# Two kept heads per task: K tiles that hold half of each head, V in 8 KB rows, V 22 positions behind

## The chip, the cores and the metric

The kernel runs on one core of a Trainium2 chip. The metric is device time in microseconds of one execution, taken as the median over several runs. Before the change it is 1160.93 us (three runs, 1159.95 to 1161.16). One execution was also recorded by the hardware profiler; that execution took 1159.96 us, and its trace spans 1157.8 us from the first to the last instruction.

A core has five engines that work side by side, each through its own instructions in order: TensorE (PE, whose weight loads are listed apart as PEld), VectorE (DVE), ScalarE (ACT), GpSimd (POOL) and SyncE (SP). SP issues every DMA of this kernel. Sixteen DMA engines carry each transfer: a tile of 128 partitions is 128 rows, eight rows to an engine, and one row that is contiguous in DRAM shows as one packet of that size.

## The reference

The reference is two layers of a decoder for one new token of each of 8 sequences. The same caches and weights serve both layers:

```python
def _A_ref(x, k_cache, v_cache, wq, wo):        # x [8,1,512], caches [8,8,8192,128] bf16
    q = (x @ wq) ...                             # 32 query heads of 128; 4 of them share a KV head
    scores = einsum("bhqd,bhkd->bhqk", q, k) * (Dh ** -0.5)
    p = softmax(scores, axis=-1)
    o = einsum("bhqk,bhkd->bhqd", p, v)
    return o.reshape(B, Sq, Hq * Dh) @ wo
def _B_ref(x, w1, w2):
    return silu(x @ w1) @ w2                     # 512 -> 1792 -> 512

x = x + _A_ref(layernorm(x), k, v, wq, wo)
x = x + _B_ref(layernorm(x), w1, w2)
x = x + _A_ref(layernorm(x), k, v, wq, wo)
x = x + _B_ref(layernorm(x), w1, w2)
```

The K cache and the V cache hold 134 MB each. Every KV head of every sequence is 2 MB of K and 2 MB of V, for 8192 keys.

## The kernel before

**Tasks and positions.** The work is cut into 128 tasks, one for each layer, sequence b and KV head g. A task has four granules k of 2048 keys; a granule of K or of V is 512 KB, that is 4 KB on each partition. The program is written out by one loop over positions `p`, eight to a task, so a granule is two positions. In each position the loop emits, in a fixed order, what is due there for several tasks at once: query preparation (`emit_q`), transposes of K (`emit_t_until`, one ahead), scores (`emit_s`), the product of probabilities and V (`emit_pv`, `LP` = 14 positions behind the scores), the steps that fold the result (`emit_own`, `emit_join`, `emit_fold`, `emit_norm`), the softmax of an earlier task in phases of its eight positions, one step of the chain that leads from one layer to the next (output projection, MLP, query projection), and at last the DMA issues that may go out (`issue_until`).

**The arena.** K and V go to an arena of `NSLOT` = 28 slots of 512 KB. `plan_loads` sorts all loads by the position that needs them and gives each a slot; `after` is the position at which the slot's old content has been used. SP issues in that order and waits before each issue until the engines have in fact let go of the slot.

**Kept heads.** `KEEP` = 20 granules, K of heads 3 to 7, are loaded once for a sequence and stay in the arena from layer 0 to layer 1. They arrive as 2 MB transfers (`READ` = 4) with 16 KB on each partition. Heads 0 to 2 are not kept: their K is loaded in both layers in 512 KB transfers. V is never kept: all of it is loaded in both layers, as 512 transfers of 512 KB with rows of 4 KB. `make_tasks` puts some five or six tasks of heads 0 to 2 (of the next sequence's layer 0, of the last sequence's layer 1) between a sequence's kept tasks of layer 0 and those of layer 1, so that the chain from layer to layer has time. While these stream, 20 of the 28 slots hold kept K.

**Scores and softmax.** After 32x32 transposes on DVE the 128 partitions are four quarters that hold different keys. The query block `QB` has 16 columns, four for each quarter, so that one pass over K gives the scores of four query heads for all quarters. The scores of a task fill one PSUM bank (`SCp`, 128 x 512). The softmax takes the row maximum (`softmax_max`), joins it over the partitions on POOL, shifts and exponentiates on ACT into `P` (`softmax_exp`), sums (`softmax_sum`), transposes `P` on PE and copies it out (`emit_pt`), each in its phase of the task that follows. `P` shares its memory, `E`, with the fold of the output (`joint`).

The lines of the profile that the text uses: L105 a wait of SP for an engine, L379 the issue of a DMA, L497 transposes of K, L563 scores, L574 row maximum, L579 join of the maximum, L586 shift, L590 exponential, L597 and L599 the sum, L608 transposes of `P`, L612 the copy out, L628 product with V, L651 and L665 the fold.

Of the kernel before, what the change touches and what calls it, by code (L numbers as in the profile page):

```python
# [19 lines left out]
READ = (1, 1, 1, 4, 4, 4, 4, 4)  # L20
KEEP = 20
LT = 1
PRE = 10
LP = 14
EARLY = 4
DEAL_AT = 30
WO_FROM = 36
NTP = 2
NSCP = 2
NPT = 1  # L30
# [12 lines left out]
NAT = 2  # L43
CW = 32
# [108 lines left out]

def make_tasks(nb, nkv, keep_from):


    first = int(keep_from)
    a = [[(0, b, g) for g in range(first)] for b in range(nb)]
    kept = [[(0, b, g) for g in range(first, nkv)] for b in range(nb)]
    c = [[(1, b, g) for g in range(first, nkv)] for b in range(nb)]  # L160
    d = [[(1, b, g) for g in range(first)] for b in range(nb)]
    ahead = [t for b in range(1, nb) for t in a[b]]
    behind = []
    tasks = a[0] + kept[0]
    na = 0
    for b in range(nb):
        if b:
            tasks += kept[b]
        size = -(-(2 * first * (nb - 1)) // nb) if b in (0, nb - 1) else 2 * first * (nb - 1) // nb
        must = max(0, first * min(b + 1, nb - 1) - na)  # L170
        nd = size if b == nb - 1 else min(len(behind), first, size - must)
        tasks += behind[:nd]
        del behind[:nd]
        take = ahead[na:na + size - nd]
        na += len(take)
        tasks += take
        if b + 1 == nb:
            tasks += behind
        tasks += c[b]
        behind += d[b]  # L180
    assert na == len(ahead)
    return tasks + d[nb - 1]


def plan_loads(tasks, kept, nslot, ngran):
# [3 lines left out]
    for i, (layer, b, g) in enumerate(tasks):  # L189
        for k in range(ngran):  # L190
# [8 lines left out]
            loads.append(Load("V", b, g, k, i0 + GPG - 1 + LP, i0 + GPG - 1 + LP))  # L199
    loads.sort(key=lambda d: (d.need, d.kind))  # L200
# [8 lines left out]
    for d in loads:  # L209
        w = ngran if d.kind == "K" and (d.g, d.k) in kept else 1  # L210
        if w > 1 and d.k:
# [9 lines left out]
        for m in range(w):  # L221
            free[d.slot + m] = d.free
        if w > 1:
            whole[d.g] = d.slot
# [19 lines left out]
def _build(ctx, nc, A_x, A_k_cache, A_v_cache, A_wq, A_wo, B_w1, B_w2, out):  # L244
# [43 lines left out]
    def half(slot, h):  # L288
# [8 lines left out]
    XT = [sb([128, KT, B], BF16, f"XT{n}") for n in range(3)]  # L297
# [5 lines left out]
    QT2 = [sb([128, HQ], BF16, "QT2") for _ in range(2)]  # L303
# [12 lines left out]
    hsT = sb([128, FT * B], BF16, "hsT")  # L316
    xnT = sb([128, KT, B], BF16, "xnT")
    s1 = sb([128, B], FP32, "s1")
    s1a = sb([128, B], FP32, "s1a")
    s2 = sb([128, 1], FP32, "s2")  # L320
    s2a = sb([128, 1], FP32, "s2a")
    top = sb([128, REP], FP32, "top")
    tops = sb([128, REP], FP32, "tops")
    ssm = [sb([128, REP], FP32, "ssm") for _ in range(NST)]
    ssa = [sb([128, REP], FP32, "ssa") for _ in range(NST)]
    widths = {"own_q": NQ, "hm": REP, "far": REP, "mine": REP, "own_x": XW, "real": 1, "rowmax": 1,
              "eps": 1, "shift": 1, "eh": FT, "vr": B, "yr": B, "tr": B}
    widths.update({f"rcp{n}": REP for n in range(NST)})
    widths.update({f"rs{n}": 1 for n in range(NST)})
    row = sb([128, sum(widths.values())], FP32, "row")  # L330
    tiny, at_col = {}, 0
    for name, w in widths.items():
        tiny[name] = row[:, at_col:at_col + w]
        at_col += w
    own_q, hm, far, mine, own_x, real, rowmax, eps, shift, vr, yr, tr = (
        tiny[n] for n in ("own_q", "hm", "far", "mine", "own_x", "real", "rowmax", "eps", "shift", "vr", "yr", "tr"))
    rcp = [tiny[f"rcp{n}"] for n in range(NST)]
    rs = [tiny[f"rs{n}"] for n in range(NST)]

# [58 lines left out]
    def issue(d):  # L398
        cache = A_k_cache if d.kind == "K" else A_v_cache
        if d.kind == "K":  # L400
            src = cache[d.b, d.g].rearrange("(p k c) d -> k p (c d)", k=NGRAN // d.wide, p=128)[d.k // d.wide]
        else:
            src = cache[d.b, d.g].rearrange("(k p c) d -> k p (c d)", k=NGRAN, p=128)[d.k]
# [7 lines left out]
    with nc.Block() as block:  # L411

        @block.sync
        def _(sync_eng):
# [13 lines left out]
                    hm[:, :], lanes.rearrange("p c (k r) -> p r c k", k=NGRAN), AX.XY, ALU.add),  # L428
                reads=["ident"], writes=["hm"],
            )  # L430
            op(
# [7 lines left out]
            for n in range(NSCP):  # L439
                op(dve, lambda n=n: dve.memset(SCp[n][:, :], 0.0), writes=[f"SC{n}"])  # L440
            op(dve, lambda: dve.tensor_reduce(real[:, :], hm[:, :], AX.X, ALU.add), reads=["hm"], writes=["real"])
# [3 lines left out]
            op(dve, lambda: dve.tensor_scalar(  # L445
                far[:, :], hm[:, :], real[:, 0:1], FAR, op0=ALU.subtract, op1=ALU.mult),
               reads=["hm", "real"], writes=["far"])
# [57 lines left out]

            span_of = {}
# [10 lines left out]
            def emit_queries(layer, b):  # L517
                if layer == 0:
                    q, rq = QT1[:, b * HQ:(b + 1) * HQ], f"QT1_{b}"
                else:  # L520
                    q, rq = QT2[b % 2][:, :], f"QT2_{b % 2}"
# [9 lines left out]
            def emit_q(ti):  # L531
                layer, b, g = tasks[ti]
                if ti == span_of[(layer, b)][0]:
                    emit_queries(layer, b)
                n = ti % NQB
                at = qset[(layer, b)] * NPART * HQ
                op(dve, lambda: dve.tensor_tensor(  # L537
                    QB[n][:, :, :].rearrange("p i (a r) -> p i a r", a=NQ),
                    QSp[:, at:at + NPART * HQ].rearrange("p (i h) -> p i h", h=HQ)[:, :, g * REP:(g + 1) * REP].unsqueeze(2)
                    .to_broadcast([128, NPART, NQ, REP]),  # L540
                    own_q[:, :].unsqueeze(1).unsqueeze(3).to_broadcast([128, NPART, NQ, REP]), ALU.mult),
                   reads=["QS", "own_q"], writes=[f"QB{n}"])

            def emit_s(i):
# [9 lines left out]
                bank, qn = ti % NSCP, ti % NQB  # L554
# [17 lines left out]
            def softmax_max(ti):  # L572
                bank = ti % NSCP
                op(dve, lambda: dve.tensor_reduce(rowmax[:, :], SCp[bank][:, :], AX.X, ALU.max),  # L574
                   reads=[f"SC{bank}"], writes=["rowmax"])
                op(dve, lambda: dve.scalar_tensor_tensor(  # L576
                    top[:, :], hm[:, :], rowmax[:, 0:1], far[:, :], op0=ALU.mult, op1=ALU.add),
                   reads=["hm", "rowmax", "far"], writes=["top"])
                op(pool, lambda: pool.partition_all_reduce(tops[:, :], top[:, :], 128, bass.bass_isa.ReduceOp.max),  # L579
                   reads=["top"], writes=["tops"])  # L580

            def softmax_shift(ti):
                op(dve, lambda: dve.scalar_tensor_tensor(  # L583
                    mine[:, :], tops[:, :], -SM_SCALE, hm[:, :], op0=ALU.mult, op1=ALU.mult),
                   reads=["tops", "hm"], writes=["mine"])
                op(dve, lambda: dve.tensor_reduce(shift[:, :], mine[:, :], AX.X, ALU.add), reads=["mine"], writes=["shift"])  # L586

            def softmax_exp(ti):
                bank, st = ti % NSCP, ti % NST
                op(act, lambda: act.activation(  # L590
                    P[:, :].rearrange("p (x j k) -> p k x j", x=CPB, k=NGRAN),
                    SCp[bank][:, :].rearrange("p (k x j) -> p k x j", k=NGRAN, x=CPB), ACT.Exp, bias=shift[:, 0:1], scale=SM_SCALE, accum_out=rs[st][:, :]),
                   reads=[f"SC{bank}", "shift"], writes=["P", f"rs{st}"])

            def softmax_sum(ti):
                st = ti % NST
                op(act, lambda: act.activation(ssm[st][:, :], hm[:, :], ACT.Copy, scale=rs[st][:, 0:1]),  # L597
                   reads=["hm", f"rs{st}"], writes=[f"ssm{st}"])
                op(pool, lambda: pool.partition_all_reduce(ssa[st][:, :], ssm[st][:, :], 128, bass.bass_isa.ReduceOp.add),  # L599
                   reads=[f"ssm{st}"], writes=[f"ssa{st}"])  # L600

            def emit_pt(ti):
                pb = ti % NPT
                tb = evacs[0] % NTP
                evacs[0] += 1
                tpv = TPp[tb][:, 0:KB].rearrange("p (c q) -> p c q", q=128)
                steps = [
                    lambda c=c: pe.transpose(tpv[:, c, :], P[:, c * 128:(c + 1) * 128], ident[:, :])  # L608
                    for c in range(CPB)
                ]  # L610
                mm_group(steps, reads=["P", "ident"], writes=[f"TP{tb}"])
                op(act, lambda: act.copy(  # L612
                    PT[pb][:, :, :, :, :].rearrange("p a t x r -> p x t a r"),
                    tpv.rearrange("p x (t q) -> p x t q", q=QUAD)[:, :, :, 0:USED].rearrange("p x t (a r) -> p x t a r", r=REP)),
                   reads=[f"TP{tb}"], writes=[f"PT{pb}"])

            def softmax_rcp(ti):
                st = ti % NST
                op(dve, lambda: dve.reciprocal(rcp[st][:, :], ssa[st][:, :]), reads=[f"ssa{st}"], writes=[f"rcp{st}"])

            def emit_pv(i):
# [3 lines left out]
                ob, pb = ti % 2, ti % NPT  # L625
# [4 lines left out]
                        PT[pb][:, k, t, y * w:(y + 1) * w].rearrange("p x r -> p (x r)"),  # L630
# [37 lines left out]
            def emit_norm(ti):  # L668
                layer, b, g = tasks[ti]
                ob, st = ti % 2, ti % NST  # L670
                if layer == 0:
                    dst, rd = at1[b % NAT][:, g * REP:(g + 1) * REP], f"at1_{b % NAT}"
                else:
                    dst, rd = at2[:, g * REP:(g + 1) * REP, b], f"QT1_{b}"
                op(dve, lambda: dve.tensor_tensor(dst, OTp[ob][:, 0:REP], rcp[st][:, :], ALU.mult),  # L675
                   reads=[f"OT{ob}", f"rcp{st}"], writes=[rd])

            def ln_stages(xv, rx, n):

                xcv, sqv, xnv = xc[:, :, 0:n], sq[:, :, 0:n], xnT[:, :, 0:n]  # L680

                def one_first():
                    op(act, lambda: act.activation(sqv, xv, ACT.Copy, scale=-1.0 / D, accum_out=s1[:, 0:1]),
                       reads=[rx], writes=["sq", "s1"])
                    op(pool, lambda: pool.partition_all_reduce(s1a[:, 0:1], s1[:, 0:1], 128, bass.bass_isa.ReduceOp.add),
                       reads=["s1"], writes=["s1a"])

                def one_second():
                    op(act, lambda: act.activation(sqv, xv, ACT.Square, bias=s1a[:, 0:1], accum_out=s2[:, 0:1]),
                       reads=[rx, "s1a"], writes=["sq", "s2"])  # L690
# [407 lines left out]
```

## Time and profile before

| | before |
|---|---|
| median of three runs | 1160.93 us |
| the profiled execution | 1159.96 us |
| its span | 1157.8 us |
| DVE busy | 740.8 us (64%) |
| PE busy | 725.2 us (63%) |
| ACT busy | 336.6 us (29%) |
| DMA, bytes | 466.80 MB |
| DMA, mean rate | 403 GB/s |

The profile page gives the busy time of each engine, then the span in 40 slices: a digit is the busy share of a slice in tenths, and the last two rows are the busy share of the 16 DMA engines and what they moved. Packets are counted by size; a packet under 512 B is the signal that ends a transfer. The chain that ended last is followed back from the last instruction to what released each step. A list of DMA issues has the time from issue to landing, which includes the queue ahead of the transfer.

### The profile page before, as it was taken

The numbers are of one execution on the slowest core, as the hardware profiler recorded it, in microseconds if no ns is written. First come the engines' busy times: TensorE is split into PE (matmuls) and PEld (weight loads), VectorE is DVE, ScalarE is ACT, GpSimd is POOL, SyncE is SP. The second block draws the span as 40 slices with busy tenths as digits, with TensorE's granted clock in tenths as the row PEclk, the third lists the DMA queues.
The fourth block names the chain that finished last, engine by engine and source line by source line (L and its number), as shares of the span: only waits on it lengthen the run. The fifth ranks groups of instructions, "written<-read, shape, count | busy, mean of one in ns | idle before, by whom it ended". The sixth has DMA issues, their size and how long they took to land.

```text
span 1157.8 us, 26616 instructions
## 1 busy us (share of the span) xinstructions
PE 725.2 (63%) x10768; PEld 346.7 (30%) x10768; DVE 740.8 (64%) x1781; ACT 336.6 (29%) x764; POOL 116.7 (10%) x296
## 2 busy tenths in 40 slices
PE   1445677566765676567756676567665677567666
PEld 1212342123322342134322342134222332134224
DVE  3836764676557675677467765677477755677464
ACT  0352224223332233122422233222332233223332
POOL 0000011001110111001100011001100011001110
PEclk9855556555765566555755576555755565556665
DMA  9999999999999999999999999999999999999994
GB/s 372 403 400 415 408 408 414 417 411 404 407 419 415 402 407 417 419 401 409 408 416 411 409 401 416 417 407 403 406 419 410 409 401 419 414 408 403 409 408 184
DMA packets 112602, 466.80 MB, mean 403 GB/s; under 512 B 11984, under 2 KB 16096, under 8 KB 106720
## 3 DMA queue, kind: packets, MB, share of 16 engines
q1 hardware_dynamic: 112480, 465.11, 100.1%
q8 instruction: 85, 1.39, 0.5%
q14 instruction: 37, 0.30, 0.1%
HBM read 465.05 MB, written 0.01 MB: 402 GB/s over the span
## 4 chain that ended last, share of the span: by engine, by line
DMA 53%; DVE 15%; PE 13%; SPq 9%; issue 6%; ACT 3%; POOL 1%; DVEq 0%; ACTq 0%; POOLq 0%
DMA arena<-in_A_v_cache_dram 36%; DMA arena<-in_A_k_cache_dram 17%; SPq L379 9%; DVE arena L497 6%; DVE E L651 4%; PE OTp L628 4%; PE SCp L563 3%; DVE row L574 2%; PE TPp L608 2%; PE OTp L665 1%; PE MISC L762 1%; ACT E L590 1%; PE MISC L780 1%; ACT PT L612 1%; DVE top L576 1%
## 5 line engine op out<-in xcount | busy, mean ns | idle before, releaser
L497 DVE STREAM_TRANSPOSE arena<-arena 128x1024 int32<-128x1024 int32 x352 | 433.3, 1235 | 162.2 <-DMA arena<-in_A_k_cache_dram 161.9
L628 PE MATMUL OTp<-arena,PT 128*16 128x512 bf16 (+1 forms) x2064 | 278.5, 550 | 292.3 <-DMA arena<-in_A_v_cache_dram 271.3
L590 ACT ACTIVATE E<-SCp,row 128x512 bf16<-128x512 f32 x128 | 181.9, 1421 | 605.9 <-DVE row L586 587.2
L563 PE MATMUL SCp<-arena,QB 128*16 128x128 bf16 (+1 forms) x4352 | 251.1, 375 | 22.6 <-DVE arena L497 16.3
L651 DVE SCALAR_TENSOR_TENSOR E<-OTp,row,E 128x128 f32<-128x128 f32 x381 | 130.2, 342 | 113.6 <-ACT E L643 103.1
L628 PEld LDWEIGHTS OTp<-arena,PT 128*16 128x16 bf16 (+1 forms) x2064 | 51.2, 92 | 422.0 <-DMA arena<-in_A_v_cache_dram 382.6
L563 PEld LDWEIGHTS SCp<-arena,QB 128*16 128x16 bf16 x4352 | 100.8, 110 | 112.2 <-issue 59.2
L579 POOL PARTITION_ALL_REDUCE tops<-top x128 | 47.5, 371 | 587.7 <-DVE top L576 439.0
L608 PE MATMUL TPp<-ident,E 128*128 128x128 bf16 x512 | 72.7, 291 | 37.6 <-ACT E L590 36.2
L599 POOL PARTITION_ALL_REDUCE ssa<-ssm x128 | 55.8, 436 | 350.2 <-ACT ssm L597 350.2
L574 DVE TENSOR_REDUCE row<-SCp 128x1 f32<-128x512 f32 x128 | 84.4, 659 | 0.7 <-PE SCp L563 0.7
L612 ACT COPY PT<-TPp 128x256 bf16<-128x256 bf16 x128 | 47.7, 372 | 125.0 <-PE TPp L608 125.0
L665 PE MATMUL OTp<-row,E 128*128 128x4 f32 x254 | 68.9, 342 | 23.3 <-DVE E L651 23.2
L665 PEld LDWEIGHTS OTp<-row,E 128*128 128x128 f32 x254 | 57.8, 283 | 82.9 <-DVE E L651 47.3
L608 PEld LDWEIGHTS TPp<-ident,E 128*128 128x128 bf16 x512 | 41.1, 124 | 111.5 <-ACT E L590 89.5
L780 PE MATMUL MISC<-at,wo 128*128 128x32 bf16 x1024 | 37.4, 188 | 18.8 <-DVE row L583 14.7
L643 ACT ACTIVATE E<-OTp,row 128x128 f32<-128x128 f32 x127 | 47.2, 372 | 0.0
L762 PE MATMUL MISC<-xnT,wq 128*128 128x32 bf16 (+1 forms) x1152 | 35.8, 186 | 14.2 <-DVE xnT L749 13.9
L762 PEld LDWEIGHTS MISC<-xnT,wq 128*128 128x128 bf16 x1152 | 34.8, 105 | 20.8 <-issue 18.6
L780 PEld LDWEIGHTS MISC<-at,wo 128*128 128x128 bf16 x1024 | 32.9, 105 | 25.4 <-DVE at L675 22.3
L597 ACT ACTIVATE ssm<-row 128x4 f32<-128x4 f32 x128 | 37.9, 296 | 3.8
L537 DVE TENSOR_TENSOR QB<-QSp,row 128x64 bf16<-128x64 f32 x128 | 25.7, 201 | 17.6 <-PE QSp L524 17.5
(100 smaller groups left out, 319.3 us busy)
## 6 DMA issues: line engine op xcount, KB each, us to landing
arena<-in_A_v_cache_dram SPq DMA_DIRECT2D x512, 512.0 KB, 10.5
arena<-in_A_k_cache_dram SPq DMA_DIRECT2D x192, 512.0 KB, 8.3
arena<-in_A_k_cache_dram SPq DMA_DIRECT2D x40, 2048.0 KB, 22.5
wq<-in_A_wq_dram SPq DMA_DIRECT2D x1, 4096.0 KB, 16.3
wo<-in_A_wo_dram SPq DMA_DIRECT2D x1, 4096.0 KB, 36.9
w<-in_B_w_dram SPq DMA_DIRECT2D x2, 1792.0 KB, 25.0
E<-in_A_x_dram SPq DMA_DIRECT2D x1, 8.0 KB
out_dram<-E SPq DMA_DIRECT2D x1, 8.0 KB
```

What stands on the lines that cost most here:

```text
L379: eng.dma_start(out_ap, in_ap).then_inc(counter.sem, 16)
L497: op(dve, lambda: dve.transpose(words, words), reads=[r_half(slot, 0), r_half(slot, 1)], writes=[r_half(slot, 0), r_half(slot, 1)])
L563: lambda n=n, t=t: pe.matmul(SCp[bank][t * QUAD:t * QUAD + USED, lo * 128:(lo + len(slots)) * 128], QB[qn][:, n, :], keys(t, n), start=(n ...
L574: op(dve, lambda: dve.tensor_reduce(rowmax[:, :], SCp[bank][:, :], AX.X, ALU.max), reads=[f"SC{bank}"], writes=["rowmax"])
L590: op(act, lambda: act.activation(P[:, :].rearrange("p (x j k) -> p k x j", x=CPB, k=NGRAN), SCp[bank][:, :].rearrange("p (k x j) -> p k x ...
L608: lambda c=c: pe.transpose(tpv[:, c, :], P[:, c * 128:(c + 1) * 128], ident[:, :])
L612: op(act, lambda: act.copy(PT[pb][:, :, :, :, :].rearrange("p a t x r -> p x t a r"), tpv.rearrange("p x (t q) -> p x t q", q=QUAD)[:, :, ...
L628: lambda t=t, y=y: pe.matmul(OTp[ob][t * QUAD:t * QUAD + w * REP, 0:w * DH], PT[pb][:, k, t, y * w:(y + 1) * w].rearrange("p x r -> p (x r)"),
L651: op(dve, lambda x=x: dve.scalar_tensor_tensor(joint, OTp[ob][:, x * DH:(x + 1) * DH], own_x[:, x:x + 1], joint, op0=ALU.mult, op1=ALU.add ...
L665: lambda: pe.matmul(OTp[ob][:, 0:REP], joint, hm[:, :], start=True, stop=True)
L762: lambda o=o, k=k: pe.matmul(MISC[:, o * n:o * n + w], w_sb[:, k, o * 128:(o + 1) * 128], rhs_of(k).to_broadcast([128, w]) if n == 1 else ...
L780: lambda o=o, h=h: pe.matmul(MISC[:, o * w:(o + 1) * w], wo_sb[:, h, o * 128:(o + 1) * 128], rhs_of(h).to_broadcast([128, w]) if n == 1 el ...
```

## The change

Heads 4 and 5, and heads 6 and 7, become pairs (`DUOS`). Heads 0 to 3 stay single, head 3 still kept.

- **K of a pair.** The two heads are 4 MB in a row in DRAM. They are read as 128 rows of 32 KB: the first 64 partitions hold head 4 (or 6), the other 64 its partner, 128 keys on each partition. The first 2 MB tile takes the first 16 KB of every row and the second the rest, so the rows are still 16 KB, now 32 KB apart.
- **V of a pair's heads.** Two granules come as one transfer of 1 MB with 8 KB on each partition, into two neighbouring slots. This makes 128 transfers out of 256.
- **Scores.** Since two quarters of the partitions belong to each head, `QB` is made by two instructions, and every K tile of a pair is scored in two groups of 16 products with 256 columns in place of one group with 512 (`score_both`). The pair fills two banks.
- **Softmax.** A pair has one softmax, after its second task: two row maxima, one join, one shift, two exponentials one after the other through the same `P`, two transposes of `P`, two copies out, one sum.
- **Order.** The softmax of every task, single ones too, comes eight positions later, and V lags 22 positions in place of 14. `DEAL_AT` and `WO_FROM` move by eight too. The query block of the first layer-1 task of a sequence is made one position before its scores (`LATE` = 4) in place of eight. `make_tasks` deals the tasks between the layers by a running due count. On equal need, V and wide K tiles now go ahead of single K granules.
- **Memory.** Three score banks and one bank for transposes of `P` in place of two and two; two buffers `PT`; the residual is updated in one buffer in place of three; small tiles are packed into `row` or into `E`.

```diff
+DUOS = (4, 6)
-LP = 14
+LP = 22
-DEAL_AT = 30
-WO_FROM = 36
-NTP = 2
-NSCP = 2
-NPT = 1
+DEAL_AT = 38
+WO_FROM = 44
+NTP = 1
+NSCP = 3
+NPT = 2
+LATE = 4
...
+def lead_of(g):
+    return g - 1 if g - 1 in DUOS else g
+
+
+def members(g):
+    return 2 if lead_of(g) in DUOS else 1
...
-            loads.append(Load("V", b, g, k, i0 + GPG - 1 + LP, i0 + GPG - 1 + LP))
-    loads.sort(key=lambda d: (d.need, d.kind))
+            w = members(g)
+            if k % w == 0:
+                loads.append(Load("V", b, g, k, i0 + GPG - 1 + LP, i0 + GPG - 1 + LP, w))
+    loads.sort(key=lambda d: (d.need, d.kind == "K" and d.wide == 1))
...
-            free[d.slot + m] = d.free
+            free[d.slot + m] = d.free + (GPG * m if d.kind == "V" else 0)
...
+        own, lead, n = d.g - lead_of(d.g), lead_of(d.g), members(d.g)
         if d.kind == "K":
-            src = cache[d.b, d.g].rearrange("(p k c) d -> k p (c d)", k=NGRAN // d.wide, p=128)[d.k // d.wide]
+            rows = cache[d.b, lead:lead + n].rearrange("g (p f) d -> (g p) (f d)", p=128 // n)
+            at = own if d.wide > 1 else d.k * n + own
+            src = rows[:, at * d.wide * SLOT:(at + 1) * d.wide * SLOT]
         else:
-            src = cache[d.b, d.g].rearrange("(k p c) d -> k p (c d)", k=NGRAN, p=128)[d.k]
+            src = cache[d.b, d.g].rearrange("(k p c) d -> k p (c d)", k=NGRAN // n, p=128)[d.k // n]
...
+            def score_both(ti, slots, qn):
+                own = tasks[ti][2] - lead_of(tasks[ti][2])
+                cols = NGRAN // 2 * 128
...
+                for u in range(2):
+                    bank = (ti - own + u) % NSCP
+                    mm_group([
+                        lambda n=n, t=t: pe.matmul(
+                            SCp[bank][t * QUAD:t * QUAD + USED, own * cols:(own + 1) * cols], QB[qn][:, n, :],
+                            many[:, u, t, n // 2, n % 2], start=(n == 0), stop=(n == NPART - 1))
+                        for n in range(NPART) for t in range(NQ)
+                    ], reads=[r_half(slot, h) for slot in slots for h in range(2)] + [f"QB{qn}"], writes=[f"SC{bank}"])
...
-            soft = {0: [softmax_max], 2: [softmax_shift, softmax_exp], 4: [softmax_sum], 5: [emit_pt], 7: [softmax_rcp]}
+            def softmax(ti, ph):
+                many = members(tasks[ti][2])
+                if ph == 0:
+                    softmax_max(ti)
+                elif ph == 2:
+                    softmax_shift(ti)
+                    softmax_exp(ti, 0)
+                elif ph == 3 and many > 1:
+                    emit_turn(ti, 0)
+                    softmax_exp(ti, 1)
+                elif ph == 4:
+                    softmax_sum(ti)
+                elif ph == 5:
+                    emit_turn(ti, many - 1)
+                    emit_pt(ti)
+                elif ph == 7:
+                    softmax_rcp(ti)
...
+            due = {GPT * t + (LATE if t in first1.values() else -LQ): t for t in turn_of if turn_of[t] is not None}
...
-                ti, ph = p // GPT - 1, p % GPT
-                if 0 <= ti < ntask and ph in soft:
-                    for f in soft[ph]:
-                        f(ti)
+                ti = p // GPT - 2
+                if 0 <= ti < ntask and lead_of(tasks[ti][2]) == tasks[ti][2]:
+                    softmax(ti, p % GPT)
```

## The prediction

> **What bounds the kernel now.** I read the page's first three parts first: which engine is full, and whether it is full all the time.
>
> ```profile
> span 1157.8 us, 26616 instructions
> PE 725.2 (63%) x10768; PEld 346.7 (30%) x10768; DVE 740.8 (64%) x1781; ACT 336.6 (29%) x764; POOL 116.7 (10%) x296
> ...
> DMA  9999999999999999999999999999999999999994
> ...
> q1 hardware_dynamic: 112480, 465.11, 100.1%
> ```
>
> No compute engine is busy for even two thirds of the span. The DMA engines are busy in every slice but the last. That alone could still be DMA engines that run while somebody else sets the pace, so the next view is who waits for whom.
>
> ```profile
> PEld OTp L628 <- DMA arena<-in_A_v_cache_dram: 382.6, 291, 16.8
> ...
> DVE arena L497 <- DMA arena<-in_A_k_cache_dram: 161.9, 83, 7.3
> ```
>
> (Columns: us in total, times, longest.) PE waits for V, and DVE for K; both are DMA. SP in turn waits for PE to free slots, but the queue never runs dry for it: counted from the issue and landing times in the trace, between 70 and 1130 us each issue makes at least 6 transfers outstanding, itself included (5 once, at 940 us). A 512 KB transfer lands every 1.28 us (median of 670 spacings; mean 1.294), so at its emptiest the queue held 5 transfers or 6.4 us of work before the next issue: a shorter stall costs nothing. The time is therefore bytes over DMA rate, plus about 2 us before the first packet and 13 us after the last V lands (1144.45 us).
>
> The rate is not the same everywhere. These are stages, 200 to 240 us with kept K tiles in the stream and 240 to 300 us without, and then the packets of two such stretches (200 to 240 and 245 to 295 us):
>
> ```profile
> 200.00:240.00 40.00, 23.15 (x216) 8.37 (x216) 26.91 (x57) 9.42 (x20) 3.20 (x8) 0.54 1.02 418
> 240.00:300.00 60.00, 40.56 (x812) 23.25 (x812) 45.34 (x101) 16.39 (x44) 6.39 (x16) 0.58 1.02 406
> ```
> ```profile
> DMA packets 2853, 16.71 MB, mean 418 GB/s; under 512 B 316, under 2 KB 316, under 8 KB 2338
> ```
> ```profile
> DMA packets 5544, 20.26 MB, mean 405 GB/s; under 512 B 615, under 2 KB 615, under 8 KB 5537
> ```
>
> Columns of the stage rows: length, busy time of PE, PEld, DVE, ACT, POOL, granted clock, DMA share, GB/s. Both stages have full DMA engines, yet the one in which 515 of the rows are 16 KB moves 3% more. A row thus has a fixed price, and that is what the change touches.
>
> **The change part by part.**
>
> *V of heads 4 to 7 in 8 KB rows.* 2 layers x 8 sequences x 4 heads x 2 transfers = 128 transfers of 1 MB, 128 rows each, 16 engines: 1024 rows of 8 KB an engine in place of 2048 of 4 KB. What one fixed price is worth comes from three readings. (a) Packet records: the median packet takes 160 ns at 4 KB, 309 ns at 8 KB (nearly all of these are wq, at the start), 615 ns at 16 KB; 2 x 160 - 309 = 11 ns a pair of rows. (b) Spacing of landings: 1.280 us for 8 rows of 4 KB an engine (160 ns each), 4.911 us for 8 rows of 16 KB (614 ns); (640 - 614) / 3 = 8.7 ns. (c) The two stretches above: 5537 - 615 = 4922 rows in 50 us x 16 is 162.5 ns; in the other, 2338 - 316 = 2022 such rows leave 311 us of engine time to 515 rows of 16 KB, 605 ns; (650 - 605) / 3 = 15 ns. Times 1024: 11.3, 8.9 and 15.4 us. I take (a), the only one that has an 8 KB row in it and the middle one: **-11.3 us**, ends -8.9 and -15.4. The 128 signals an engine fewer (median 9 ns, 1.2 us) stay within these ends.
>
> The Trainium skill (DMA: Bandwidth & Descriptors, "Why small descriptors are slow") puts the overhead of a packet at about 3 cycles against one per 32 B. As an estimate from that page, 131 cycles become 129.5 for each 4 KB, 1.1% of the 331 us (256 x 1.294) that this V takes now, or 3.8 us. The records of this trace show 11 ns where that would be 3.7, and the sum goes by the records.
>
> *K of the pairs.* Rows stay 16 KB, bytes and count (32 pairs' worth of 2 MB tiles) stay, the pitch goes from 16 to 32 KB. The trace has no 32 KB pitch. Nearest: narrow K rows (4 KB at 16 KB pitch) against V rows (4 KB without gap) show a spacing of 1.280 us for both and mean records of 163.3 and 163.8 ns. So **0**; the ends are 0 and a twentieth of the tile's 4.91 us, +0.25 x 32 = +8 us, which I hold unlikely.
>
> *DMA order and slots.* Both old and new lag are even and fall on the same phase of a task, so while heads 0 to 2 stream, one K and one V slot still come free at each odd position. A V pair takes its second half two positions early and waits for two neighbouring slots, which lowers the lead by one or two transfers: from 6.4 to 3.8 us at the least. **0** as long as stalls are shorter than this; beyond it they count in full. SP issues 128 transfers fewer (0.33 us each, off the path), so nothing queues longer behind it.
>
> *Scores of a pair.* 64 tasks x 16 more products. PE pays 36 ns net for 128 columns (111.8 us / 3072) and 109 ns for 512 (139.3 / 1280); a line between gives 60 ns for 256, so 32 x 60 - 16 x 109 = +0.2 us a task, 13 us in all, on a PE idle for 17 of 40 us in that stage. **0**.
>
> *Softmax of a pair.* In series: two maxima 1.32, combining 0.15, L576 0.22, POOL 0.37, shift 0.31, exponential 1.69, transposes 0.6, exponential 1.69, transposes 0.6, copies 0.74: 7.7 us. A layer-1 pair has 4 MB of V, some 10 us, a layer-0 pair 20 us with its K. New is that PE sits in phase 3 behind the first exponential and in phase 5 behind the second; before it waited 3.4 us in four such waits of the 200 to 240 us stage. At up to 3.4 us a pair, four pairs a sequence, that is 14 us in the 77 us of a sequence's kept work (40 V transfers x 1.294 + 5 K tiles x 4.96 mean), of which PE is idle for 40%. Late next would be V products, which release slots; the count outstanding there is 8 to 12 transfers. **0**; uncovered it would be 3.4 x 32 = +109 us. DVE and ACT lose work (32 sums, shifts and joins fewer).
>
> *Eight positions more of lag, `LATE`.* The layer chain starts 8 positions later and its deadline moves by 7: from 19 to 18 positions (with five tasks between). The first layer-1 query block is made one position before its scores, so PE waits for QT2, the query products and one 0.2 us DVE product: perhaps 1.5 us, eight times, under the 3.8 us lead. **0**; uncovered +12 us.
>
> *Start and end.* The first 28 slots fill with more K before V; the runway (28 slots, wq, w1, wo: 66.8 us) and the heads that free the first 12 slots are the same: 0, give or take one spacing of 1.3 us. At the end the last tasks are single heads, and softmax against V product has the same distance: 0, give or take 1.3 us.
>
> Sum: 1159.96 - 11.3 = 1148.7 us for the profiled execution, which lay 0.97 us under the median: **1149.6 us**.
>
> **The rivals.**
>
> 1. *Smaller gain: the fixed price is partly hidden already.* Queue 1's packets took 100.1% of the span, though data flowed only from about 2 to 1144 us: records overlap by some 2%, 3.4 ns of 160. Reading (b) less that is 5.3 ns, 5.4 us: 1155.5 us. The page's three cycles (3.8 us, estimate) would give 1157. Against it: (b) is a spacing and contains no overlap.
> 2. *No change: K at 32 KB pitch costs the gain.* 0.35 us on each of 32 tiles, 7%, would do: 1161 us. The Trainium skill (same page, "Latency and other measured facts") tells of copies of 16 KiB rows that slow down at pitches of large powers of two, from 512 KiB on, far beyond this one; no run here shows it. Against: the narrow K at four times its row length is as fast as V. That the rows never become 8 KB is excluded by the source pattern.
> 3. *Slower: the first layer-1 scores come late.* The chain, with one position fewer, then waits for `emit_q` right before the scores; PE stands, no slot comes free, the queue runs dry. The lead covers 3.8 us; each us beyond costs 8 us a run (eight sequences), so it has eaten the gain at 5.2 us. At 7 us late: (7 - 3.8) x 8 = +26, 1175 us. For it: PE's steps in this chain are strictly in order. Against: the same chain's waits today are 3.0 us for L812 and 1.1 us for L847 a sequence.
>
> **How the numbers follow.** Forecast 0.72 (own range 1146 to 1153), rival 1 0.07, rival 2 0.07, rival 3 and what resembles it 0.14. A difference of 0.2% (2.3 us) is about the least a measurement of this kernel can tell from none. Faster: the forecast and 0.05 of rival 1, 0.77. Same: the rest of rival 1, where less than 2.3 us is left, and 0.06 of rival 2, 0.08. Slower: rival 3 and 0.01 of rival 2, 0.15. The range goes from reading (c) with 1 us to either side, 1145, to rival 1 and the near half of rival 2, 1160: about 0.8.
>
> **What would show it.** Right: 16384 packets of 8 KB with a median near 309 ns and 32768 fewer of 4 KB; 414 GB/s or more over the kept stages with the DMA row still 9 throughout; unchanged rates near 405 in the single-head stages; the last V landing near 1133 us; a tail of 13 us. Wrong: a digit below 9 in the DMA row at the turn from layer 0 to 1 (rival 3), wide K landing over 5.1 us apart (rival 2), 8 KB packets above 315 ns (rival 1).

## The result: slower, although the rows cost less

The changed kernel takes 1178.47 us (median of 4 runs, 1174.75 to 1180.24) against 1161.05 us before: ratio 1.0148, 95% interval 1.0134 to 1.0162. The profiled execution took 1179.96 us, its trace spans 1178.2 us. The forecast was 1149.6 us.

Parts 1 to 3 of the profile page after the change:

```profile
span 1178.2 us, 28178 instructions
...
DMA  9999999999999999999999999999999999999992
...
DMA packets 94175, 466.90 MB, mean 396 GB/s; under 512 B 9936, under 2 KB 14048, under 8 KB 71904
...
q1 hardware_dynamic: 94048, 465.10, 98.5%
```

The rows did change as the diff says: packets under 8 KB fell from 106720 to 71904. The bytes are the same and the mean rate is lower. In slices of 29 us every DMA digit is still 9, so the page alone hides what happened. A finer look at one turn from kept heads to single heads shows it. First the DMA digits of 105 to 135 us (40 slices of 0.75 us), then 100 to 140 us as one stage, after the change and before it (last three columns: granted clock, DMA share, GB/s):

```profile
DMA  9999998494999999989987979999899999999989
```
```profile
100.00:140.00 40.00, 22.27 (x400) 12.13 (x400) 27.59 (x50) 6.88 (x14) 1.60 (x4) 1.00 0.97 367
```
```profile
100.00:140.00 40.00, 24.31 (x396) 12.25 (x396) 29.37 (x62) 10.29 (x26) 3.98 (x10) 0.50 1.02 408
```

The clock does not explain the drop: it was higher after the change in this stretch. The DMA engines run short, for a few us at a time, near the start of each stretch of single heads. To add this up, give every packet of queue 1, which carries the data, its price (16 KB 614 ns, 14 KB 540, 8 KB 310, 4 KB 160, 3.5 KB 142, 1 KB 50.5, a signal 9; medians of the records) and divide by 16. What of the first 1140 us is not paid for is DMA time lost, the start of some 2 to 4 us and the instruction fetches of the other two queues (0.6% of the span) included; the rest of the span, beyond price and loss, is the end.

| profiled execution | price of all packets | lost by 1140 us | end | span |
|---|---|---|---|---|
| before | 1136.1 | 6.0 | 15.7 | 1157.8 |
| after | 1124.7 | 32.4 | 21.1 | 1178.2 |

So 11.4 us were won at the rows, 26.4 us more were lost, and the end grew by 5.4 us: +20.4 us in all. The loss, called gaps below, has two faces in the packet records up to 1140 us. Packets of 4, 8 and 16 KB whose record is over 1.5 times the price add 25.9 us (1356 packets) in place of 8.7 us (472); what such a packet waited for, the records do not say. And the time in which fewer than 16 packets are on record adds up to 13.7 us of all engines in place of 5.6. Each row of the table is one execution, and executions of one kernel lie up to 9 us apart, so a few us in this account tell nothing; the medians do.

Lines of the changed kernel: L107 a wait of SP, L516 transposes of K, L638 shift, L642 exponential, L655 a pair's sum, L667 transposes of `P`, L709 product with V. The chain of waits turned too. After the change:

```profile
DVE arena L516 <- DMA arena<-in_A_k_cache_dram: 127.5, 85, 19.6
...
PEld OTp L709 <- DMA arena<-in_A_v_cache_dram: 46.9, 25, 13.3
```

PE's weight loads waited 382.6 us for V before, 46.9 us now: V lies in its slots earlier than PE can use it, and holds them. That alone is not what empties the queue: the kernel with V in 512 KB (below), which has few of the gaps, shows 46.7 us. From 70 to 1130 us the fewest outstanding transfers at an issue, itself included, fell from 6 (once 5) to 3 or 4 in every sequence.

### The profile page after: what moved, and what is told of

Same layout as the page of the kernel before. It is cut to its first block, busy times and chain, and to the rows that moved or that the text cites. A ratio compares the mean times of both kernels' runs of the same rounds, so it can differ in the third digit from the quotient of the medians.

```text
span 1178.2 us, 28178 instructions
## 1 busy us (share of the span) xinstructions
PE 701.5 (60%) x11792; PEld 378.9 (32%) x11792; DVE 739.7 (63%) x1719; ACT 315.8 (27%) x700; POOL 91.0 (8%) x232
## 4 chain that ended last, share of the span: by engine, by line
DMA 34%; DVE 23%; PE 18%; issue 13%; ACT 8%; SPq 3%; POOL 2%; DVEq 0%; ACTq 0%; POOLq 0%
DMA arena<-in_A_k_cache_dram 34%; DVE arena L516 8%; DVE E L732 7%; ACT E L642 5%; PE SCp L578 4%; PE OTp L709 4%; DVE row L620 4%; SPq L394 3%; PE TPp L667 3%; PE SCp L606 2%; PE MISC L851 2%; ACT PT L674 1%; PE OTp L746 1%; ACT E L724 1%; POOL row L629 1%
## 5 line engine op out<-in xcount | busy, mean ns | idle before, releaser
L516 DVE STREAM_TRANSPOSE arena<-arena 128x1024 int32<-128x1024 int32 x352 | 430.6, 1232 | 128.3 <-DMA arena<-in_A_k_cache_dram 127.5
L642 ACT ACTIVATE E<-SCp,row 128x512 bf16<-128x512 f32 x128 | 180.8, 1413 | 516.0 <-DVE row L638 434.3
L709 PE MATMUL OTp<-arena,PT 128*16 128x512 bf16 (+1 forms) x2064 | 275.2, 562 | 54.1 <-DMA arena<-in_A_v_cache_dram 36.0
L606 PE MATMUL SCp<-arena,QB 128*16 128x128 bf16 (+1 forms) x3328 | 138.9, 314 | 106.9 <-DVE arena L516 92.6
L667 PE MATMUL TPp<-ident,E 128*128 128x128 bf16 x512 | 75.1, 299 | 124.5 <-ACT E L642 124.1
L578 PE MATMUL SCp<-arena,QB 128*16 128x256 bf16 x2048 | 113.3, 387 | 46.5 <-DVE arena L516 29.7
L606 PEld LDWEIGHTS SCp<-arena,QB 128*16 128x16 bf16 x3328 | 68.9, 109 | 173.4 <-DVE arena L516 142.5
L667 PEld LDWEIGHTS TPp<-ident,E 128*128 128x128 bf16 x512 | 42.5, 127 | 193.3 <-ACT E L642 171.0
L746 PEld LDWEIGHTS OTp<-row,E 128*128 128x128 f32 x254 | 55.1, 271 | 120.6 <-DVE E L732 107.4
L578 PEld LDWEIGHTS SCp<-arena,QB 128*16 128x16 bf16 x2048 | 60.3, 115 | 94.0 <-DVE arena L516 46.2
L629 POOL PARTITION_ALL_REDUCE row<-row x96 | 36.1, 376 | 700.9 <-DVE row L626 587.9
L709 PEld LDWEIGHTS OTp<-arena,PT 128*16 128x16 bf16 (+1 forms) x2064 | 58.2, 108 | 92.2 <-DMA arena<-in_A_v_cache_dram 46.9
L674 ACT COPY PT<-TPp 128x256 bf16<-128x256 bf16 x128 | 44.5, 373 | 88.5 <-PE TPp L667 88.4
L658 POOL PARTITION_ALL_REDUCE row<-row x96 | 41.5, 432 | 298.0 <-ACT row L652 140.6
L655 DVE SCALAR_TENSOR_TENSOR row<-row 128x8 f32<-128x8 f32 x32 | 7.3, 228 | 87.5 <-ACT E L642 87.5
L642 ACT ACTIVATION_READ_ACCUMULATOR E<-SCp,row 128x1 f32 x128 | 33.5, 262 | 0.0
```

Source lines behind the costliest of these rows:

```text
L516: op(dve, lambda: dve.transpose(words, words), reads=[r_half(slot, 0), r_half(slot, 1)], writes=[r_half(slot, 0), r_half(slot, 1)])
L578: lambda n=n, t=t: pe.matmul(SCp[bank][t * QUAD:t * QUAD + USED, own * cols:(own + 1) * cols], QB[qn][:, n, :], many[:, u, t, n // 2, n % ...
L606: lambda n=n, t=t: pe.matmul(SCp[bank][t * QUAD:t * QUAD + USED, lo * 128:(lo + len(slots)) * 128], QB[qn][:, n, :], keys(t, n), start=(n ...
L642: op(act, lambda: act.activation(P[:, :].rearrange("p (x j k) -> p k x j", x=CPB, k=NGRAN), SCp[bank][:, :].rearrange("p (k x j) -> p k x ...
L674: op(act, lambda: act.copy(PT[pb][:, :, :, :, :].rearrange("p a t x r -> p x t a r"), tpv.rearrange("p x (t q) -> p x t q", q=QUAD)[:, :, ...
L709: lambda t=t, y=y: pe.matmul(OTp[ob][t * QUAD:t * QUAD + w * REP, 0:w * DH], PT[pb][:, at, t, y * w:(y + 1) * w].rearrange("p x r -> p (x ...
```

## The experiments

Theories: S, the 1 MB V pairs take slots that the queue needs; C, the compute chain of a pair makes scores and releases late; L, the lag of 22 positions itself; O, the order of K and V on equal need. The first expectation says P for the pairs as a whole, S and C together. "Lost" is DMA time lost by 1140 us in the profiled execution. Unless said otherwise an edit is made to the changed kernel alone.

**No pairs, lag kept.**

```diff
-DUOS = (4, 6)
+DUOS = ()
```

> The changed kernel with no pairs at all: every head single, V in 512 KB transfers with 4 KB rows, but the softmax and V still as late as in the change (22 positions). Cost of the bytes by packet prices: 1136 us as before the change, 11.4 us more than with 8 KB rows. If the pairs cause the dry queue (theory P), the queue stays full and only the longer tail (about 5 us) remains: 1164 to 1168 us. If the lag and the order around it cause it (theory L), the 26 us stay and the dearer rows come on top: 1186 to 1192 us.

Measured: 1163.4 us, ratio 1.0021 (1.0012 to 1.0030). Lost 9.8 us, end 14.8 us. Theory L falls: lag, late query, order on a tie and the packed memory together cost 2.8 us of medians. The longer end is not the lag's either.

**Pairs, but V in 512 KB.**

```diff
-            w = members(g)
-            if k % w == 0:
-                loads.append(Load("V", b, g, k, i0 + GPG - 1 + LP, i0 + GPG - 1 + LP, w))
+            loads.append(Load("V", b, g, k, i0 + GPG - 1 + LP, i0 + GPG - 1 + LP))
```

with a source of 4 KB rows taken out of the 8 KB pattern.

> The changed kernel with pairs in K, scores and softmax, but V of the pairs in 256 transfers of 512 KB with 4 KB rows, each needed at its own position. If what empties the queue is that a 1 MB V transfer takes two neighbouring slots of the 8 that are free (theory S), most of the 26 us of lost DMA time go and 11.4 us of dearer rows come: 1162 to 1170 us, issues at the start of the single heads again with 6 or more transfers outstanding. If it is the compute chain of the pair (theory C: DVE behind the sum, PE behind two exponentials), the loss stays: 1186 to 1192 us.

Measured: 1170.0 us, 1.0081 (1.0066 to 1.0096). Lost 13.6 us, end 18.9 us, at a price of 1136.1 us. The same stretch of this kernel:

```profile
100.00:140.00 40.00, 24.02 (x426) 13.17 (x426) 29.54 (x57) 6.90 (x14) 1.97 (x5) 0.50 1.02 404
```

Back from 367 to 404 GB/s, with the compute of the pairs unchanged. In this stretch SP waits for V products of PE, first in the changed kernel, then here, where the same line is L708 (us in total, times, longest):

```profile
SPq L107 <- PE OTp L709: 17.8, 7, 6.4
```
```profile
SPq L107 <- PE OTp L708: 7.3, 3, 2.8
```

Rows that are 11.4 us dearer make the kernel 8.5 us faster, so the 1 MB V transfers cost 19.9 us. Against the kernel without pairs, the pairs' scores and softmax cost 6.6 us.

**The pair's sum two phases later.**

```diff
-                elif ph == 4:
+                elif ph == 4 and many == 1:
                     softmax_sum(ti)
...
+                elif ph == 6 and many > 1:
+                    softmax_sum(ti)
```

> The changed kernel with the sum of a pair, which runs on DVE and waits there for the second exponential with the transposes of K behind it, moved from phase 4 to phase 6. If this wait (87.5 us in 32 times, 2.7 us each) is what makes scores and slots late (theory C), the DVE wait at the sum falls below 20 us and the loss of DMA time from 26 to 10 us or less: 1160 to 1166 us. If the slots are the cause (theory S), the wait goes and the time stays: 1175 to 1180 us.

Measured: 1176.7 us, 1.0129 (1.0109 to 1.0149); lost 35.2 us. The sum of a pair in the groups of this kernel, then of the changed one (busy, mean ns, idle time before and its releaser):

```profile
L655 DVE SCALAR_TENSOR_TENSOR row<-row 128x8 f32<-128x8 f32 x32 | 7.3, 228 | 59.1 <-ACT E L642 59.1
```
```profile
L655 DVE SCALAR_TENSOR_TENSOR row<-row 128x8 f32<-128x8 f32 x32 | 7.3, 228 | 87.5 <-ACT E L642 87.5
```

The wait shrank by a third, less than expected, since DVE's queue has little between the two places, and the lost time did not shrink. The 28 us of this wait that went bought nothing; the 59 us that stay are not tested here.

**K ahead of V on equal need.**

```diff
-    loads.sort(key=lambda d: (d.need, d.kind == "K" and d.wide == 1))
+    loads.sort(key=lambda d: (d.need, d.kind))
```

> The changed kernel with the loads sorted as before the change: on equal need K goes ahead of V. If K singles land too late behind 1 MB of V (theory O: order), DVE's wait for K (127 us) falls and 5 to 15 us come back: 1163 to 1174 us. By theories S and C the order on a tie moves one transfer by one place and the time stays: 1175 to 1181 us.

Measured: 1173.0 us, 1.0108 (1.0091 to 1.0126); lost 25.0 us. Theory O holds for a part: 7 us of gaps in the trace, 5.5 us of medians.

**Pairs 3+4 and 5+6.**

```diff
-DUOS = (4, 6)
+DUOS = (3, 5)
```

> The changed kernel with the pairs moved by one head: 3+4 and 5+6, and head 7 alone as the last kept head. Bytes and rows are the same (packet prices 1124.7 us). The softmax of the last pair now falls into the kept work, and of the slots that the plan fills ahead of need in the first two single-head tasks 6.1 and 6.6 are left on average in place of 6.0 and 6.1 (7.0 before the change). Theory C (the pair's softmax at the start of the single heads makes scores late): the loss of DMA time falls from 26 us over that of before to under 12: 1160 to 1166 us. Theory S (slots): it falls only in part, to 15 to 22 us: 1168 to 1176 us.

Measured: 1200.8 us, 1.0347 (1.0331 to 1.0362), lost 56.6 us. Both theories missed. The trace has a single outstanding transfer at the worst of every sequence and the DMA at or near zero for 2 to 3 us. In one such place PE finishes V products at 642.7 us and starts the next at 649.7: the pair's softmax now falls just where K of head 7, 2 MB that lands as a whole, and V pairs fill the slots. That these meet there is seen; that the meeting is the whole cause is argued.

**One pair, 4+5.**

```diff
-DUOS = (4, 6)
+DUOS = (4,)
```

> The changed kernel with one pair, 4+5; heads 6 and 7 are single. Half of the 8 KB rows stay: 1130.4 us by packet prices. V of the pair is nearly used up when the single heads start. Theory S: the loss of DMA time falls to 4 to 10 us over that of before, and the tail to 2 to 4 us more: 1162 to 1169 us. Theory C by number of pairs: half of the loss stays, 13 us, and the tail: 1170 to 1176 us.

Measured: 1163.0 us, 1.0026 (1.0014 to 1.0037); lost 12.9 us. Half of the pairs, but a quarter of the added gaps: this points to the pair next to the single heads (the run with V of 6+7 in 512 KB, below, says the same of its V alone).

**Twelve free slots in place of eight.**

```diff
-KEEP = 20
+KEEP = 16
```

> The changed kernel with head 3 no longer kept (16 granules kept in place of 20): four slots more are free while the single heads stream, 12 in place of 8, for 16.8 MB more of K, some 43 us by packet prices (1167 to 1168 us in all). The plan then fills 10 slots ahead in the first single tasks in place of 6. Theory S: DMA time lost before 1140 us falls to 10 us or less (before the change 6, changed kernel 32): 1195 to 1203 us. Theory C: it stays at 20 to 32 us: 1207 to 1222 us.

Measured: 1198.7 us, 1.0330 (1.0309 to 1.0351), with 43 us more of bytes. Lost by 1140 us: 11.2 us. Both pairs, their softmax and all 1 MB transfers are there, and most of the gaps are gone (the kernel without pairs loses 9.8 us):

```profile
100.00:140.00 40.00, 22.35 (x396) 11.39 (x396) 27.10 (x53) 6.91 (x14) 1.97 (x5) 0.54 1.02 412
```

With slots enough, neither the pairs' V nor their compute empties the queue, as S has it. The 43 us of added bytes also give the compute more DMA time to hide behind, so this run alone does not part S from C; the run with V in 512 KB, at the same compute and eight free slots, does.

**V of 4+5 in 1 MB, of 6+7 in 512 KB, K first.**

```diff
-            w = members(g)
+            w = members(g) if lead_of(g) == DUOS[0] else 1
...
-    loads.sort(key=lambda d: (d.need, d.kind == "K" and d.wide == 1))
+    loads.sort(key=lambda d: (d.need, d.kind))
```

> The changed kernel with both pairs, V of pair 4+5 in 1 MB transfers and V of pair 6+7 in 512 KB transfers, and K ahead of V on equal need. 1130.4 us by packet prices; V in 1 MB is nearly used up when the single heads start, so by theory S the lost DMA time is 8 to 14 us and the tail some 4 us longer than before the change: 1160 to 1168 us. By theory C it keeps 25 us of loss: 1173 to 1180 us.

Measured: 1163.7 us, 1.0032 (1.0020 to 1.0043); lost 11.5 us. As S has it; the edit changes the order on a tie as well, and the run does not part the two. (The 512 KB pieces are taken out of the 8 KB pattern here too.)

**Second half early, but in 512 KB** (on the kernel with all V in 512 KB).

```diff
-            loads.append(Load("V", b, g, k, i0 + GPG - 1 + LP, i0 + GPG - 1 + LP))
+            early = GPG * (k % members(g))
+            loads.append(Load("V", b, g, k, i0 + GPG - 1 + LP - early, i0 + GPG - 1 + LP))
```

> As e2_v_512k (all V in 512 KB transfers, 4 KB rows), but the second half of each V pair is due two positions early, as it is in a 1 MB transfer. The plan then fills 6.5 slots ahead in the first two single-head tasks (e2: 7.0; changed kernel: 6.0 and 6.1). If holding a slot two positions longer is what empties the queue, the DMA time lost before 1140 us is 18 to 28 us (e2: 13.6; changed kernel: 32.4): 1174 to 1184 us. If it is the wait for two neighbouring slots and the landing of 1 MB as a whole, it stays near e2: 1168 to 1173 us.

Measured: 1178.1 us, 1.0147 (1.0126 to 1.0168), 8.1 us over the kernel that it is made from, at the same bytes and rows; lost 18.5 us in the profiled execution, which at 1174.6 us was the quickest of the four. Holding 512 KB two positions longer is a real cost.

**One pair and K first.**

```diff
-DUOS = (4, 6)
+DUOS = (4,)
...
-    loads.sort(key=lambda d: (d.need, d.kind == "K" and d.wide == 1))
+    loads.sort(key=lambda d: (d.need, d.kind))
```

> One pair, 4+5, with V in 1 MB transfers, heads 6 and 7 single, and K ahead of V on equal need: e6_pair_4 and e4_k_first together. 1130.4 us by packet prices, 12.9 us lost in e6. If the order on a tie costs DMA time as it did with two pairs (7 us there), 3 to 5 us come back: 1157 to 1161 us. If it only matters behind 1 MB transfers in the single-head work, of which there are few here: 1162 to 1164 us.

Measured: 1162.2 us, 1.0008 (0.9999 to 1.0017), lost 13.3 us: no difference from before that can be told. The order on a tie gives next to nothing where few 1 MB transfers stand among the single heads.

**The query block earlier.**

```diff
-LATE = 4
+LATE = 0
```

> The changed kernel with the query block of the first layer-1 task made five positions before its scores in place of one (LATE = 0; the layer chain then has 14 positions in place of 18). If the late query (rival 3 of the prediction) costs DMA time, 5 to 15 us come back: 1163 to 1173 us. If the slots do, nothing changes or the shorter chain costs a little: 1176 to 1182 us.

Measured: 1180.4 us, 1.0171 (1.0154 to 1.0189); lost 31.9 us. The late query is not the cause.

**1 MB everywhere but for 6+7 in layer 0, K first.**

```diff
-            w = members(g)
+            w = members(g) if layer or lead_of(g) == DUOS[0] else 1
...
-    loads.sort(key=lambda d: (d.need, d.kind == "K" and d.wide == 1))
+    loads.sort(key=lambda d: (d.need, d.kind))
```

> As e8_first_pair_8k, but V of pair 6+7 also comes in 1 MB transfers in layer 1, where it is used up before single heads follow; in layer 0 it stays in 512 KB transfers. 1127.6 us by packet prices, 2.8 us under e8. By theory S the lost time stays at 10 to 14 us: 1159 to 1163 us. If 1 MB transfers cost wherever they are: 1165 to 1172 us.

Measured: 1162.9 us, 1.0016 (1.0008 to 1.0025); lost 14.8 us, just above what S gave. Of the 2.8 us in price little is left, and no version beats the kernel before.

**The plan of the pairs, landings of 512 KB.**

```diff
+        if d.kind == "V" and d.wide > 1:
+            syn.acquire(sp, writes=[r_half(d.slot + m, h) for m in range(d.wide) for h in range(2)])
+            for m in range(d.wide):
+                dma(sp, ARENA[:, (d.slot + m) * SLOT:(d.slot + m + 1) * SLOT], src[:, m * SLOT:(m + 1) * SLOT],
+                    slsem[d.slot + m], writes=[r_half(d.slot + m, h) for h in range(2)])
...
```

> The changed kernel with the same plan of slots and the same waits: a V pair still waits until two neighbouring slots are free and is due as a pair, but is then issued as two 512 KB transfers with 4 KB rows that land and are waited for one by one (1136 us by packet prices; SP issues 128 more). If the plan (neighbours, second half early) is the cause, the DMA time lost before 1140 us stays near 32 us and the dearer rows come on top: 1186 to 1192 us. If the landing of 1 MB as a whole is what costs beyond the early second half, it falls to that of e9 (18.5 us): 1174 to 1180 us.

Measured: 1195.1 us, 1.0296 (1.0257 to 1.0335), above both ranges; lost 40.1 us. Its stretch:

```profile
100.00:140.00 40.00, 20.41 (x392) 11.73 (x396) 25.69 (x49) 6.38 (x13) 1.60 (x4) 0.54 0.97 359
```

The landing as a whole was not to blame: without it the loss stays, and is somewhat larger. Against the kernel with all V in 512 KB this one differs in the plan and the wait alone and is 25.1 us slower. Of this, the early second half is 8.1 us; the other 17 us come, by subtraction, with the wait for two neighbouring slots and what it delays in SP's queue. The plan is thus shown to be enough for the loss; how its two parts work together is not.

## Why the prediction was wrong

*V in 8 KB rows, -11.3 us: right.* Median records after the change are 159 ns at 4 KB and 311 ns at 8 KB (before: 160 and 309), 7 to 11 ns a pair of rows; by the prices above, signals included, the change is worth 11.4 us. The three cycles that the Trainium skill gives (DMA: Bandwidth & Descriptors, "Why small descriptors are slow"), 3.7 ns in the prediction's estimate, are less than either reading.

*K at 32 KB pitch, 0: right.* The median 16 KB packet takes 614 ns after and 615 ns before. Rival 2 has no ground.

*DMA order and slots, 0: this is the step that failed.* It priced the V pair at one or two transfers of lead, held that the 3.8 us left cover any stall in sight, and so put the term at 0. The runs put 19.9 us there. The plan loses what was foreseen: it fills 6.0 and 6.1 slots ahead in the first two single-head tasks in place of 7.0. But 3.8 us stands for three 512 KB transfers ahead of an issue, and at the worst there were two. At the first turn five issues from 105.6 us on bring 3.1 MB in 10.3 us, with a stop of 4.3 us among them, where 4.2 MB could have flowed at 405 GB/s; ahead of the next issue, at 115.9 us, stand two transfers of 512 KB, or 2.6 us. Before the change a stop of 10.6 us ends at 103.6 us with 3.7 MB still ahead of the issue; from there to 136 us no stop is over 3.4 us and at least 2.6 MB, five transfers, stand ahead of each issue. With V in 512 KB at least four transfers stand there from 105 to 135 us.

A second reason makes 3.8 us too little, and it is argued. The lead was counted to the landing of a transfer, which is the last of its 16 signals. In the trace of before, the first signal comes 3.5 us ahead of the last (mean; 2.5 to 4.5 for nine in ten), and at the shortest 2.8 us pass from an issue to the first signal. An engine that is ahead can thus be out of work while the slowest still has work for 3 us. The sign was on view in the trace of before, where at the end the rate faded from 287 GB/s at 1140 to 1141 us to 86 at 1143 to 1144 us, and the busy share of the engines from 0.71 to 0.24. How much of the loss is this drift and how much the shorter supply, no run tells apart. That slots set the loss is shown, by the runs with V in 512 KB, with the second half early, and with the plan alone; the run with twelve free slots agrees.

*The order on a tie* was in the diff, and the prediction gave it no term of its own; with two pairs it is worth 5.5 us, with one next to nothing.

*Softmax and scores of a pair, 0: wrong by 6.6 us* (kernel with V in 512 KB against the one without pairs: 3.8 us of gaps, 4.1 us of end in the profiled executions). The serial length was summed fairly, but laid beside DMA time. While layer-1 heads run, V is in hand and the order of the instructions sets the pace; that this is where the 6.6 us go is read from the trace and tested by no run. A pair there in the timeline of the changed kernel:

```profile
985.63 1.39 ACT L642 ACTIVATE E<-SCp,row 128x512 bf16<-128x512 f32 x1 [4.04 <-DVE row L638]
...
987.08 0.61 PE L667 MATMUL TPp<-ident,E 128*128 128x128 bf16 x4 [3.09 <-ACT E L642]
...
989.29 0.63 PE L709 MATMUL OTp<-arena,PT 128*16 128x512 bf16 x4
...
989.86 0.61 PE L667 MATMUL TPp<-ident,E 128*128 128x128 bf16 x4
...
990.98 1.03 PE L709 MATMUL OTp<-arena,PT 128*16 128x512 bf16 x8 [0.51 <-issue]
```

(Start, length, engine and line, idle time before and what ended it.) PE stands 3.1 us behind the first exponential, and when its V product at last comes it waits for no DMA.

*Lag and `LATE`, 0: 2.8 us with all else that e1 keeps.* Rival 3 had the sign and nearly the time (1175), but that was luck: an earlier query block gave nothing.

*The end, 0 +- 1.3: 5.4 us longer.* In the changed kernel the last V lands at 1159.4 us. The transposes of the last three softmaxes:

```profile
1149.49 0.61 PE L667 MATMUL TPp<-ident,E 128*128 128x128 bf16 x4
...
1155.35 0.61 PE L667 MATMUL TPp<-ident,E 128*128 128x128 bf16 x4 [0.73 <-ACT E L642]
...
1161.19 0.61 PE L667 MATMUL TPp<-ident,E 128*128 128x128 bf16 x4 [0.73 <-ACT E L642]
```

They are 5.8 us apart, a pace of compute, and the last comes after the last V has landed. Before, the last one was at 1140.77 us, with 3.7 us of V still to land. PE came to the last heads late: the last K lands at 1142.9 us and is scored at 1150.0. Without pairs the end is 14.8 us, with one 17.0 and 18.7, with two 17.4 to 21.1 (one execution each); that the layer-1 pairs' pace makes it late is argued from this.

Taken in this order the medians split the 17.9 us (1178.5 less 1160.6, before's median in those runs) like this: +2.8 for lag, order and memory, +6.6 for the pairs' compute, +19.9 for V in pairs of slots, -11.4 for the rows. The split between the last two rests on the packet prices.

## What to carry to other kernels

A DMA-bound kernel whose buffers are nearly full pays for every buffer held longer; price a larger transfer by the lead it takes from the queue where free buffers are fewest, before its cheaper rows. Measure lead to the first signal of a transfer, and take off the time from issue to that; the landing flatters it by the engines' drift (3.5 us here). And put off no compute for the sake of DMA without following it to the end of the program, where nothing hides it.

## What the runs showed of the hardware

The 16 signals of one transfer come apart, and further apart with a deeper queue: from first to last 3.5 us on average before, 2.4 us after the change with its shorter queue, 5.6 us with twelve free slots. A queue that shows three transfers outstanding can leave engines idle: in 105 to 135 us of the changed kernel the rate was 354 GB/s with 3 to 6 outstanding at each issue. Long packet records go with a short queue as well: of the packets of 4 KB and more in the changed kernel (70 to 1130 us), 3.5% took over 1.5 times their price where three transfers were outstanding, 0.8% where seven were.
